# Fifty steps of a hand-written order put elsewhere, in a kernel that joins linear attention to a squared-ReLU layer

## The chip, the core and the metric

The kernel runs on one core of a Trainium2 chip. The core has five engines that work at the same time, each through its own queue in program order: TensorE (PE in the profile, its weight loads PEld), VectorE (DVE), ScalarE (ACT), GpSimd (POOL) and SyncE (SP), which here only issues DMAs. They wait for one another by semaphores. The metric is the time on the device in microseconds, lower is better.

## The reference

```python
# r, k, v: [4 batches, 8 heads, 768 steps, 48];  w, u: [8, 48]
for t in range(S):
    cur = einsum('bhd,bhe->bhde', u * k[t], v[t])
    y[t] = einsum('bhd,bhde->bhe', r[t], state + cur)
    state = w * state + einsum('bhd,bhe->bhde', k[t], v[t])
x = y.transpose(0, 2, 1, 3).reshape(3072, 384)
h = maximum(x @ w_in, 0)          # w_in  384 x 2048
out = (h * h) @ w_out             # w_out 2048 x 384
```

A recurrence over 768 steps gives 3072 rows of 384 numbers; each row then goes through two matrix products with a squared ReLU between them. Inputs and output are float32; the kernel multiplies in bf16.

## The kernel before

**Units and groups.** The recurrence is cut into 24 units, each 128 steps of one batch with all 8 heads (`UNITS` gives batch and chunk). Inside a unit it is done with matrix products, from unit to unit of a batch by a carried state. Units go in pairs through the dense layer: group g holds units 2g and 2g+1, except that units 22 and 23 are the groups 11 and 12 alone.

**Steps.** All work is a list of some 950 steps in one string, `ORDER`. A step is written `name.unit:engine/buffers`; `F1.8.2:P/1` is step F1 of group 8, slice 2, on TensorE into PSUM bank 1. The letters are P TensorE, D VectorE, A ScalarE, G GpSimd, S SyncE. A loop walks through the string and issues each step to its engine. So the string sets the order in each queue; between the queues only data, buffers and semaphores count. The steps that matter here, by unit i or group g:

- `ld.r`, `ld.k`, `ld.v` (L328): DMAs that bring 192 KB each. `rh`, `kh` (L347, L344): r and k times powers of w, in bf16. `XB` (L411): both transposed by a DMA.
- `P0`, `P1`, `du`, `dv` (L350, L354, L357, L362): the products r k, times u, summed over a head, times v: the term `cur`. `vb` (L259 or L257): v in bf16.
- `A` (L418): one product per head, eight matmuls of 48 rows, into two banks. `Bm` (L426): one of these banks times the mask, to SBUF.
- `Y` (L486 state part, L488 in-unit part): the output of the unit, in one bank. `xs` (L519): that plus dv, to bf16. `X` and `xTc` (L533, L257/L259), or the DMA `xX` (L540): xs transposed, x for the dense layer.
- `U`, `ts`, `S` (L508, L525, L528): the next state. `S` overwrites `S0W`, the state in bf16 of that batch, which `Y` of the same unit reads.
- `F1.g.s` (L549): six or twelve matmuls from x of the group into one bank. `re` (L571 on ScalarE, L573 on VectorE): ReLU of that bank into one of six `hr` buffers. `sq` (L578, L580): its square into one of 28 `hq` buffers.
- `F2.i.q` (L589): four matmuls from two squares of the group; four of them, q = 0 to 3, make the output of unit i in one bank. `os` copies it to SBUF, `out` writes it (L642). Unit 23 is done in two halves, `Fh`, `oh`, `outh` (L603, L257, L617).

**Buffers.** PSUM has 8 banks; a step that writes a bank waits until the step that reads what stood there is done. The same holds for `hr`, `hq`, `rk` and all the others; the number behind the slash says which buffer of its kind a step takes.

```python
    for step in ORDER.split():
        ...
        for h, j in zip(held, given):
            slot[h] = int(j)
        getattr(Do, name)(E[eng], *at)
```

Of the kernel before, what the change touches and what calls it, by code (L numbers as in the profile page):

```python
# [71 lines left out]
rh.17:G/1 F2.10.1:P/6 re.5.4:A/2 xs.12:D/2 xX.12:S/2 F2.11.0:P/2 os.9:D/1 sq.5.4:A/21 P0.16:G/0 XB.17:S/3 ts.13:D/1
Y.13:P/1 kh.16:D/5 F2.10.3:P/6 rh.16:G/5 F2.10.2:P/6 xs.13:D/3 out.5:S du.15:D/4 ld.k.18:S/4 F2.10.0:P/6 P1.16:G
ld.r.21:S/3 A.15:P/7/5 A.14:P/0/3 ld.r.19:S/2 Bm.15.0:D/5 dv.15:G F2.11.1:P/2 ld.r.18:S/5 Bm.15.1:D/7 S.13:G X.13:P/7
F2.11.3:P/2 xTc.13:A/2 Bm.14.0:D/4 Y.15:P/5 vb.14:G/7 du.14:D/0 F1.6.3:P/1 kh.19:G/0 xs.15:D/4 xX.15:S/0 ld.v.16:S/1
F1.6.2:P/7 re.6.3:A/0 Bm.14.1:D/6 F1.6.6:P/0 out.9:S out.6:S os.8:D/3 re.6.2:A/1 ld.r.20:S/4 sq.6.3:D/17 Y.14:P/5
re.6.6:A/3 P0.21:G/3 dv.14:D du.17:D/2 F1.6.1:P/1 XB.16:S/2 os.10:A/4 F1.6.4:P/4 S.12:G xs.14:D/0 F1.6.5:P/7
ld.k.20:S/5 rh.19:G/0 U.15:P/0 F1.6.7:P/6 re.6.5:A/4 ld.v.17:S/0 ts.15:D/1 X.14:P/3 S.15:G F1.6.0:P/5 re.6.7:A/5
xTc.14:D/0 P0.19:D/2 sq.6.2:A/20 sq.6.6:A/22 F1.7.7:P/7 XB.19:S/4 F1.7.6:P/0 re.6.4:D/2 sq.6.7:A/23 U.14:P/6 rh.21:G/3
out.8:A F1.7.5:P/3 re.7.6:D/0 kh.18:G/4 ld.r.23:S/6 vb.16:A/1 du.16:D/3 F1.7.0:P/4 sq.6.5:A/24 rh.20:G/6 re.6.0:D/1  # L80
F1.7.2:P/0 re.7.7:A/3 rh.18:D/4 ld.v.19:S/3 sq.6.4:A/25 F1.7.4:P/5 re.7.2:A/5 sq.7.2:A/5 F2.13.3:P/7 re.7.4:D/4
# [15 lines left out]
F1.9.2:P/7 re.9.2:A/2 du.22:D/2 F1.9.7:P/5 sq.9.6:A/12 du.21:D/1 F2.17.3:P/2 out.15:G out.12:G re.9.7:A/1 dv.21:G
F2.17.0:P/2 sq.9.3:A/15 vb.22:D/7 dv.23:G re.9.5:A/3 Y.20:P/7 Bm.21.0:D/2 F1.9.1:P/5 re.9.4:A/5 dv.22:D S.19:G
sq.9.5:A/8 F2.17.2:P/2 xs.20:D/0 sq.9.2:A/21 sq.9.4:D/17 Y.21:P/1 xX.20:S/0 sq.9.0:A/20 F2.17.1:P/2 xs.21:D/1
sq.9.7:A/7 F2.19.1:P/3 re.9.1:A/0 xX.21:S/0 F2.18.2:P/6 os.17:A/3 sq.9.1:A/9 A.23:P/0/7 A.22:P/1/5 os.16:A/0  # L100
Bm.23.0:D/4 F2.18.1:P/6 Bm.22.0:D/7 F2.18.3:P/6 Bm.22.1:D/5 F2.18.0:P/6 F2.19.0:P/3 Y.22:P/4 F1.10.2:P/2 re.10.2:D/3
# [5 lines left out]
sq.11.2:A/25 F1.10.7:P/6 re.10.6:A/3 F2.22.2:P/0 sq.10.6:A/4 re.10.7:D/2 re.12.0:A/5 F2.20.2:P/1 sq.11.1:D/5
sq.10.7:D/10 sq.12.0:A/14 F1.12.3:P/7 sq.12.1:D/18 F2.20.3:P/1 re.12.3:A/0 F2.20.0:P/1 Fh.23.2.0:P/4 os.20:A/5
# [585 lines left out]
```

## Time and profile before

| what | value |
| --- | --- |
| runs shown | 168.78, 169.06, 170.26 us, median 169.06 |
| the profiled execution | 168.3 us, of which span 166.5 us |
| busy, share of the span | PE 96%, DVE 79%, ACT 62%, POOL 60% |
| granted clock of TensorE | 1.0 throughout |
| instructions | 4501 |

The span runs from the first to the last recorded instruction. The views used: the page (busy shares, 40 slices, the chain that ended last), the timeline of one engine (start and length of each instruction or run of like ones, in brackets the idle time ahead of it and what ended it), and the table of stretches (columns: length, then busy time of PE, PEld, DVE, ACT, POOL with the number of instructions in brackets, then clock, DMA share, GB/s; of a single line it gives PE and PEld alone). An instruction belongs to a step by its place in its engine's order; `x12` in a row of L589 is three F2 steps.

### The profile page before, as it was taken

To read this page: it belongs to the slowest core of one execution; us is meant where nothing else is said; L and a number is where in the kernel's file an instruction comes from. 1 tells how busy PE (TensorE), PEld (TensorE's weight loads), DVE (VectorE), ACT (ScalarE), POOL (GpSimd) and SP (SyncE) were. 2 spreads that over 40 slices of the span, in tenths; PEclk is the share of its full clock that TensorE was granted. 3 is DMA by queue.
4 is the path that set the end of the run, shared out by engine and by line. 5 is a ranking of instruction groups with operands and counts; after the bars stand their busy time and mean duration, and the time that the engine had idled before them with its cause. 6 is when DMAs were issued, how large, how long until landed. Compare 5 with 4: busy or idle time off the path is not lost.

```text
span 166.5 us, 4501 instructions
## 1 busy us (share of the span) xinstructions
PE 160.1 (96%) x1772; PEld 120.4 (72%) x1772; DVE 132.3 (79%) x254; ACT 102.6 (62%) x193; POOL 100.3 (60%) x124
## 2 busy tenths in 40 slices
PE   4898999999999999999999999999999999999993
...
PEclk9999999999999999999999999999999999999999
...
GB/s 131 322 234 192 201 186 198 206 204 172 178 194 201 164 188 200 171 187 193 179 220 127 221 215 186 201 214 183 200 147 139 241 78 22 66 127 0 2 144 96
DMA packets 97713, 28.02 MB, mean 168 GB/s; under 512 B 92538, under 2 KB 97404, under 8 KB 97692
## 3 DMA queue, kind: packets, MB, share of 16 engines
...
q0 software_dynamic: 3072, 4.33, 13.2%
q10 hardware_dynamic: 892, 1.18, 3.1%
q8 instruction: 14, 0.23, 0.5%
q14 instruction: 7, 0.06, 0.1%
...
## 4 chain that ended last, share of the span: by engine, by line
PE 91%; DMA 4%; DVE 1%; ACT 1%; issue 1%; ACTq 0%; DVEq 0%
PE bank L549 37%; PE bank L589 35%; PE bank L418 3%; DMA xT<-xs 2%; PE bank L488 2%; DMA urow<-in_u_dram 2%; PE bank L486 2%; PE bank L371 2%; PE bank L533 2%; PE bank L603 2%; PE bank L508 1%; DVE Bm L399 1%; PE bank L278 1%; PE bank L561 1%; PE bank L391 1%; PE bank L405 1%
## 5 line engine op out<-in xcount | busy, mean ns | idle before, releaser
L589 PE MATMUL bank<-W,hq 128*128 128x384 bf16 x368 | 68.4, 326 | 0.0
L549 PE MATMUL bank<-xT,W 128*128 128x256 bf16 (+1 forms) x612 | 68.3, 264 | 0.1
L571 ACT ACTIVATE hr<-bank 128x512 bf16<-128x512 f32 x68 | 39.4, 594 | 35.1 <-PE bank L549 33.4
L549 PEld LDWEIGHTS <-W 128*128 128x128 bf16 x612 | 54.8, 98 | 8.4 <-issue 0.4
L589 PEld LDWEIGHTS <-hq 128*128 128x128 bf16 x368 | 33.7, 98 | 18.7
L578 ACT ACTIVATE hq<-hr 128x512 bf16<-128x512 bf16 x70 | 40.9, 626 | 5.6 <-DVE hr L573 4.7
L426 DVE TENSOR_TENSOR Bm<-bank,maskJT 128x512 bf16<-128x512 f32 x40 | 25.4, 679 | 2.8 <-PE bank L418 2.8
L573 DVE TENSOR_SCALAR hr<-bank 128x512 bf16<-128x512 f32 x28 | 18.7, 682 | 7.3 <-PE bank L549 4.8
L354 POOL TENSOR_TENSOR P<-P,ub 128x384 f32<-128x384 f32 x15 | 16.4, 1095 | 9.1 <-DVE P L350 8.7
L362 POOL TENSOR_TENSOR dv<-ldv,du 128x384 f32<-128x384 f32 (+1 forms) x18 | 15.7, 886 | 7.4 <-issue 3.8
L347 POOL TENSOR_TENSOR rk<-ldr,Wt 128x384 bf16<-128x384 f32 x15 | 15.6, 1043 | 2.2 <-DMA ldr<-in_r_dram 2.2
L580 DVE TENSOR_TENSOR hq<-hr 128x512 bf16<-128x512 bf16 x26 | 14.2, 560 | 2.3 <-ACT hr L571 2.1
L350 POOL TENSOR_TENSOR P<-ldr,ldk 128x384 f32<-128x384 f32 x13 | 13.3, 1023 | 2.6 <-DMA ldr<-in_r_dram 1.4
L344 POOL TENSOR_TENSOR rk<-ldk,Wk 128x384 bf16<-128x384 f32 x12 | 12.4, 1039 | 2.8 <-DMA ldk<-in_k_dram 2.3
L357 DVE TENSOR_REDUCE du<-P 128x8 f32<-128x384 f32 x24 | 12.8, 542 | 1.0 <-POOL P L354 0.9
L519 DVE TENSOR_TENSOR xs<-bank,dv 128x384 bf16<-128x384 f32 x20 | 10.9, 550 | 2.0 <-POOL dv L362 0.7
L259 POOL CAST vb<-ldv 128x384 bf16<-128x384 f32 x10 | 6.3, 626 | 10.3 <-DMA ldv<-in_v_dram 10.3
L528 POOL TENSOR_TENSOR S0W<-ts,WLm 128x384 bf16<-128x384 f32 x10 | 10.6, 1062 | 1.0 <-DVE ts L525 0.9
L259 DVE COPY os<-bank 128x384 f32<-128x384 f32 x11 | 6.0, 550 | 6.5 <-PE bank L589 6.3
L525 DVE TENSOR_TENSOR ts<-bank,S0W 128x384 f32<-128x384 f32 x16 | 8.8, 549 | 2.4 <-PE bank L508 1.1
L488 PE MATMUL bank<-vb,Bm 128*128 128x48 bf16 x160 | 9.5, 183 | 0.0
L488 PEld LDWEIGHTS <-Bm 128*128 128x128 bf16 x160 | 8.2, 96 | 1.3 <-DVE xs L519 0.4
(90 smaller groups left out, 166.5 us busy)
## 6 DMA issues: line engine op xcount, KB each, us to landing
...
```

The costliest lines, as they stand in the source:

```text
L347: e.tensor_mul(rk[slot[f"rk{i}"]][:, 0, :, 0:D], loaded("r", i), Do.factor("t", i % 2 if i < PAIRED else 2))
L350: e.tensor_mul(P0b[slot[f"P{i}"]], loaded("r", i), loaded("k", i))
L354: e.tensor_mul(t, t, bank("bu")[:, 0 : H * D].rearrange("p (h d) -> p h d", h=H) if i in EARLY_U else ub)
L362: e.tensor_mul(dv_of(i) if i < PAIRED else dvb[slot[f"dv{i}"]], loaded("v", i), t)
L426: e.tensor_mul(Bmb[slot[f"Bm{i}{h}"]], heads(bank(f"bA{i}{h}"), 128), mask_b)
L488: e.matmul(y[:, hc, D * h : D * (h + 1)], m[h][:, hc, :], vb[:, 2 * hc + h, :], start=(c == 0), stop=True, skip_group_check=True,)
L549: e.matmul(hp[:, fi, :], W1[f // 4][:, c, 256 * (f // 2 % 2) : 256 * (f // 2 % 2 + 1)].rearrange("p (m j) -> p j m", j=2)[:, f % 2, :], xt ...
L571: e.activation(hr, hp, AF.Relu)
L573: e.tensor_scalar_max(hr, hp, 0.0)
L578: e.activation(hq, hr, AF.Square)
L580: e.tensor_mul(hq, hr, hr)
L589: e.matmul(bank(f"bO{i}")[:, 0:d_model], hqb[slot[f"hq{g},{f // m}"]][:, at : at + L], W2[q][:, f % 4, :], start=(seen[i] == 1 and f % 4 = ...
```

## The change

Steps stand at other places in the string, three are on another engine, and some have other banks. No step is added or taken away, no function is changed. What each queue sees:

- **TensorE**: F2.3.2 ahead of Y.4; U.7 ahead of F2.5.1; F2.5.2 and F1.3.3 ahead of F1.3.1; A.10 from ahead of A.8 to behind X.9; F2.7.2 ahead of F2.7.0; Y.10 ahead of X.11; U.16 later, behind F1.7.1, and A.17 right after it, F2.12.1, F1.7.3 and F2.13.0 between it and A.16; F2.12.2 and F1.8.7 ahead of F1.8.2; F2.16.0 between A.20 and A.21; A.22 ahead of A.23; F1.10.2 ahead of F2.19.0, F1.10.5 earlier; F1.10.4, F1.10.6 and F2.20.1 ahead of F1.11.1, F1.11.2 earlier; Fh.23.3.0 ahead of Fh.23.1.1.
- **VectorE**: xs.4 ahead of du.5; S0.4 behind os.1; du.7 ahead of os.3; S.6 ahead of P0.10; xs.11 ahead of P1.13; du.13, S.8, xs.13, Bm.15.1, du.17, sq.6.0, P0.18, du.23 and xs.22 elsewhere by a step or a few; vb.17 ahead of sq.7.6 and ts.16.
- **ScalarE**: sq.0.1, re.4.3 and sq.4.1 come from VectorE; sq.3.7 from behind re.3.5 to behind sq.3.6.
- **GpSimd**: kh.13 from behind dv.9 (ahead of S.9) to behind P0.13; vb.12 ahead of S.10; S.11 behind dv.13; rh.17, rh.16; kh.18 ahead of S.15, P1.19 behind it; rh.20 and P1.18 behind P0.20; dv.18 ahead of vb.20, P1.20 behind it; P1.23 ahead of P1.22; dv.23 and out.15 ahead of vb.21.
- **SyncE**: the same order.

The core of the diff, places cut out:

```diff
-Y.4:P/0 P1.5:G du.5:D/0 F2.3.2:P/6 sq.1.2:A/15 ld.v.7:S/6 ld.k.9:S/0 xs.4:D/4 F2.0.0:P/4 vb.5:A/5 F2.3.0:P/6 Y.5:P/0
+F2.3.2:P/6 Y.4:P/0 P1.5:G sq.1.2:A/15 ld.v.7:S/6 ld.k.9:S/0 xs.4:D/4 du.5:D/0 F2.0.0:P/4 vb.5:A/5 F2.3.0:P/6 Y.5:P/0
...
-Bm.9.0:D/3 ld.v.12:S/4 dv.9:G sq.3.5:A/7 Bm.11.1:D/5 F1.3.6:P/0 Bm.11.0:D/7 sq.3.4:A/3 du.8:D/4 kh.13:G/4 A.10:P/5/7
-A.8:P/4/6 re.3.6:A/5 F2.7.0:P/2 Bm.8.0:D/0 sq.3.6:A/9 ld.k.12:S/5 ld.r.15:S/7 Y.9:P/1 vb.11:A/2 F2.7.2:P/2 Bm.8.1:D/1
-dv.8:D S.9:G vb.10:A/3 ld.k.14:S/7 F2.6.3:P/3 out.4:A P1.10:G Y.8:P/4 xs.9:D/3 F2.7.3:P/2 U.10:P/0 xs.8:D/4 P0.13:G/0
-X.9:P/6 Bm.10.1:D/4 X.8:P/1 F2.6.2:P/3 xTc.8:A/0 xTc.9:D/0 du.11:D/0 rh.12:G/0 Y.11:P/4 du.10:D/2 dv.10:G out.0:S
-F1.4.7:P/7 dv.11:G Bm.10.0:D/6 F1.4.6:P/6 ld.v.13:S/5 re.4.7:A/0 P1.13:D ld.r.14:S/6 F1.4.3:P/1 xs.11:D/0 re.4.6:A/1
-ld.v.15:S/6 du.13:D/1 F2.7.1:P/2 rh.15:G/6 ld.k.15:S/6 ts.10:D/1 F1.4.4:P/5 re.4.4:A/4 XB.13:S/5 kh.12:G/0 X.11:P/7
-Y.10:P/6 F1.4.1:P/4 S.10:G xs.10:D/1 sq.4.4:A/4 F1.4.5:P/5 re.4.3:D/3 ld.k.17:S/0 sq.4.6:D/2 X.10:P/0 F1.4.0:P/1
...
+ld.v.12:S/4 dv.9:G sq.3.5:A/7 Bm.11.1:D/5 F1.3.6:P/0 Bm.11.0:D/7 sq.3.4:A/3 du.8:D/4 A.8:P/4/6 re.3.6:A/5 F2.7.2:P/2
+F2.7.0:P/2 Bm.8.0:D/0 sq.3.6:A/9 sq.3.7:A/5 ld.k.12:S/5 ld.r.15:S/7 Y.9:P/1 vb.11:A/2 Bm.8.1:D/1 dv.8:D S.9:G
+vb.10:A/3 ld.k.14:S/7 F2.6.3:P/3 out.4:A P1.10:G Y.8:P/4 xs.9:D/3 F2.7.3:P/2 U.10:P/0 xs.8:D/4 P0.13:G/0 kh.13:G/4
+X.9:P/6 A.10:P/5/7 Bm.10.1:D/4 X.8:P/1 F2.6.2:P/3 xTc.8:A/0 xTc.9:D/0 du.11:D/0 rh.12:G/0 Y.11:P/4 du.10:D/2 dv.10:G
+out.0:S F1.4.7:P/7 dv.11:G Bm.10.0:D/6 F1.4.6:P/6 ld.v.13:S/5 re.4.7:A/0 xs.11:D/0 P1.13:D ld.r.14:S/6 F1.4.3:P/1
+re.4.6:A/1 ld.v.15:S/6 F2.7.1:P/2 rh.15:G/6 ld.k.15:S/6 ts.10:D/1 F1.4.4:P/5 re.4.4:A/4 XB.13:S/5 kh.12:G/0 Y.10:P/6
+X.11:P/7 F1.4.1:P/4 xs.10:D/1 sq.4.4:A/4 F1.4.5:P/5 re.4.3:A/3 ld.k.17:S/0 sq.4.6:D/2 X.10:P/0 F1.4.0:P/1 xTc.10:A/1
...
-XB.18:S/1 F2.11.2:P/2 ts.14:D/0 re.7.0:A/2 sq.6.0:D/9 U.16:P/0 F2.13.2:P/7 re.7.5:A/5 P1.21:D re.6.1:A/1 P0.18:D/4
-F1.7.1:P/5 sq.7.6:D/3 sq.6.1:A/7 ld.v.18:S/2 ld.v.20:S/5 P1.18:G F2.12.1:P/6 vb.17:D/0 sq.7.7:A/26 F1.7.3:P/4
-re.7.1:A/0 P1.19:G F2.13.0:P/7 ts.16:D/1 sq.7.0:A/27 sq.7.1:D/0 ld.v.21:S/4 re.7.3:A/1 A.17:P/3/1 dv.16:G A.16:P/5/0
...
+XB.18:S/1 F2.11.2:P/2 ts.14:D/0 re.7.0:A/2 F2.13.2:P/7 re.7.5:A/5 re.6.1:A/1 P0.18:D/4 F1.7.1:P/5 U.16:P/0 sq.6.1:A/7
+ld.v.18:S/2 ld.v.20:S/5 A.17:P/3/1 F2.12.1:P/6 P1.21:D vb.17:D/0 sq.7.6:D/3 sq.7.7:A/26 F1.7.3:P/4 re.7.1:A/0 P1.19:G
+rh.21:G/3 F2.13.0:P/7 ts.16:D/1 sq.7.0:A/27 sq.7.1:D/0 ld.v.21:S/4 re.7.3:A/1 dv.16:G A.16:P/5/0 Bm.17.1:D/2
...
-U.18:P/7 Y.18:P/0 S.17:D F1.8.2:P/1 du.18:D/4 F2.12.2:P/6 dv.18:G ts.19:D/0 F1.8.7:P/3 xs.19:D/3 xX.19:S/2 P0.23:G/0
+U.18:P/7 Y.18:P/0 S.17:D du.18:D/4 F2.12.2:P/6 dv.18:G vb.20:G/4 P1.20:G ts.19:D/0 F1.8.7:P/3 F1.8.2:P/1 xs.19:D/3
...
-A.20:P/1/5 S.18:G A.21:P/6/2 Bm.20.1:D/1 Bm.20.0:D/0 F2.16.0:P/4 vb.21:G/6 kh.22:D/5 Bm.21.1:D/3 F2.16.1:P/4 XB.22:S/2
+re.9.6:A/5 ts.18:D/1 A.20:P/1/5 S.18:G Bm.20.1:D/1 Bm.20.0:D/0 F2.16.0:P/4 A.21:P/6/2 kh.22:D/5 Bm.21.1:D/3 du.22:D/2
...
-re.10.5:D/5 Y.23:P/4 sq.10.5:D/22 F2.19.2:P/3 xs.23:D/3 re.10.3:A/4 sq.10.3:A/23 xX.23:S/1 sq.10.2:A/0 F1.11.1:P/7
-out.17:G F1.11.0:P/6 F1.10.4:P/0 out.16:G re.11.1:D/1 F2.21.1:P/5 re.11.0:A/0 F1.10.6:P/4 re.10.1:A/5 sq.11.0:D/27
-re.10.4:D/4 F1.11.3:P/2 sq.10.1:D/1 sq.10.4:A/6 F1.12.1:P/7 re.11.3:D/3 F1.11.2:P/6 sq.11.3:D/3 F2.20.1:P/1
...
+re.10.5:D/5 Y.23:P/4 sq.10.5:D/22 F2.19.2:P/3 xs.23:D/3 re.10.3:A/4 sq.10.3:A/23 xX.23:S/1 sq.10.2:A/0 F1.10.4:P/0
+F1.10.6:P/4 F2.20.1:P/7 F1.11.1:P/6 out.17:G F1.11.0:P/5 out.16:G re.11.1:D/1 F1.11.2:P/2 F2.21.1:P/6 re.11.0:A/0
+re.10.1:A/5 sq.11.0:D/27 re.10.4:D/4 F1.11.3:P/5 sq.10.1:D/1 sq.10.4:A/6 F1.12.1:P/1 re.11.3:D/3 sq.11.3:D/3
```

More of the change, by code (lines that the diff above doesn't have):

```diff
@@ L72 @@
[L72 to L81, printed above, removed]
@@ L97 @@
[L97 to L101, printed above, removed]
@@ L107 @@
[L107 to L110 removed]
+A.9:P/6/4 A.11:P/1/2 P0.11:D/2 P1.11:G sq.3.2:A/27 F2.6.0:P/3 ld.r.12:S/4 Bm.9.1:D/2 re.3.5:A/3 F2.6.1:P/3 Bm.9.0:D/3
```

76 lines of the change are left out of this document (46 added, 30 removed).

## The prediction

> **What bounds the kernel now.** I read the page first, then the table of stretches, then TensorE's timeline step by step.
>
> ```profile
> PE 160.1 (96%) x1772; PEld 120.4 (72%) x1772; DVE 132.3 (79%) x254; ACT 102.6 (62%) x193; POOL 100.3 (60%) x124
> PE   4898999999999999999999999999999999999993
> PEclk9999999999999999999999999999999999999999
> PE 91%; DMA 4%; DVE 1%; ACT 1%; issue 1%; ACTq 0%; DVEq 0%
> 64.00:72.00 8.00, 8.00 (x99) 6.40 (x97) 7.25 (x15) 3.30 (x7) 7.36 (x9) 1.00 0.79 169
> ```
>
> TensorE is busy 96% of the span at a full clock, its idle slices are the first few and the last one, and 91% of the chain is its own work. So the end moves by what happens to TensorE's queue: waits that close, waits that open, and work that becomes dearer. The other engines matter only where TensorE waits for them.
>
> The busy share hides short waits, since a matmul is drawn for some 0.2 us after it starts and covers the gap behind it. So I go by starts, from one step to the next.
>
> ```profile
> 44.77 1.46 PE L589 MATMUL bank<-W,hq 128*128 128x384 bf16 x8
> 46.07 1.63 PE L549 MATMUL bank<-xT,W 128*128 128x256 bf16 x12
> ```
>
> Two F2 steps of four matmuls take 46.07 - 44.77 = 1.30 us, 0.65 each. Against this price three places stand out after 25 us (before that only one square and one bank are changed).
>
> ```profile
> 33.75 2.11 PE L589 MATMUL bank<-W,hq 128*128 128x384 bf16 x12
> 35.88 0.37 PE L488 MATMUL bank<-vb,Bm 128*128 128x48 bf16 x8
> ...
> 34.80 0.55 DVE L357 TENSOR_REDUCE du<-P 128x8 f32<-128x384 f32 x1 [0.94 <-POOL P L354]
> 35.27 0.55 DVE L519 TENSOR_TENSOR xs<-bank,dv 128x384 bf16<-128x384 f32 x1
> ...
> 116.67 0.21 PE L486 MATMUL bank<-S0W,rkT 128*128 128x96 bf16 x1
> 117.29 0.55 PEld L549 LDWEIGHTS <-W 128*128 128x128 bf16 x6 [0.20 <-DMA xT<-xs]
> ...
> 144.27 0.81 PE L589 MATMUL bank<-W,hq 128*128 128x384 bf16 x4
> 145.08 2.15 PE L549 MATMUL bank<-xT,W 128*128 128x128 bf16 x30
> ```
>
> **The change: waits that close.** (1) F2.3.2, F2.0.0 and F2.3.0 should take 3 x 0.65 = 1.95 us, but Y.5 begins 35.88 - 33.75 = 2.13 after the first: it waited 0.18. It writes bank 0, which xs.4 has to read first, and xs.4 ends at 35.27 + 0.55 = 35.82 because it stands in VectorE's queue behind du.5, which sat 0.94 until GpSimd's P1.5. The change puts xs.4 ahead of du.5, and F2.3.2 ahead of Y.4. Y.4's results then come at about 34.6, xs.4 ends near 35.2, and Y.5 arrives at 35.70. **-0.18.** The next that is late is F1.2.5 behind os.2; it keeps its place and its wait.
>
> (2) Y.18 begins at 116.67; a Y step takes 0.37 (below, 71.17 to 71.54), so F1.8.2 should start at 117.04. It starts at 117.29, and the row names the transpose that brings x of 16/17. The change puts F2.12.2 (0.65) ahead of the first F1 of that group, more than the wait. **-0.25.**
>
> (3) F2.19.2 takes 145.08 - 144.27 = 0.81 instead of 0.65: F1.11.1 waits for x of 22. Now F1.10.4, F1.10.6 and F2.20.1 go first (two times 0.655, by the 12 matmuls from 71.54 to 72.85 below, and 0.65), and xs.22 goes ahead of re.10.2 on VectorE, so that its transpose is issued earlier too. F2.20.1's squares sq.10.2 and sq.10.3 are ready before it by the same order of queues. **-0.16.**
>
> **Work that becomes dearer.** A.10 leaves A.8, A.17 leaves A.16, and F2.16.0 goes between A.20 and A.21. In the trace every A stands beside another one.
>
> ```profile
> 81.20 1.46 PE L589 MATMUL bank<-W,hq 128*128 128x384 bf16 x8
> 82.59 0.62 PE L418 MATMUL bank<-rkT 48*128 48x128 bf16 x16
> 83.15 1.80 PE L589 MATMUL bank<-W,hq 128*128 128x384 bf16 x10
> ...
> 82.59:82.83 0.24, 0.23 (x9) 0.24 (x10) 1.00 0.93 160
> 82.83:83.15 0.32, 0.32 (x14) 0.21 (x8) 1.00 0.96 194
> ```
>
> The two F2 steps ahead of a pair take 82.59 - 81.20 = 1.39 instead of 1.30: a run-in of 0.09. Of the pair's 0.56 the first A takes 0.24 and the second 0.32 (the last two rows count L418 alone; weights are loaded in only 0.21 of the second stretch): a run-out of 0.08. The pair pays both once. Apart, each A pays them: 0.17 per pair split, three pairs, **+0.51.** No lone A of this form is in the trace, so the ends are 0 (a pair's cost stays a pair's) and 0.6.
>
> The Trainium skill's page "TensorEngine Tiling (Array Packing)", Key Properties, says that a change of the tiling mode, not of the tile alone, drains TensorE; an A has 48 rows where its neighbours have 128. By that rule every lone A drains twice and the sum is the +0.51; without it, it would be 0. The two gaps in the rows agree with it.
>
> **A wait that opens.** kh.13 goes from before S.9 to behind P0.13 in GpSimd's queue, and Y.10 goes ahead of X.11 on TensorE.
>
> ```profile
> 61.72 0.83 POOL L362 TENSOR_TENSOR dv<-ldv,du 128x384 f32<-128x384 f32 x1
> 63.05 1.00 POOL L344 TENSOR_TENSOR rk<-ldk,Wk 128x384 bf16<-128x384 f32 x1 [0.50 <-PE bank L418]
> 64.12 1.00 POOL L528 TENSOR_TENSOR S0W<-ts,WLm 128x384 bf16<-128x384 f32 x1
> 65.08 1.32 POOL L354 TENSOR_TENSOR P<-P,ub 128x384 f32<-128x384 f32 x1
> 68.33 1.93 POOL L362 TENSOR_TENSOR dv<-ldv,du 128x384 f32<-128x384 f32 x2
> ...
> 62.28 0.62 PE L418 MATMUL bank<-rkT 48*128 48x128 bf16 x16
> 63.49 0.21 PE L486 MATMUL bank<-S0W,rkT 128*128 128x96 bf16 x1
> 63.82 0.21 PE L488 MATMUL bank<-vb,Bm 128*128 128x48 bf16 x2
> 71.00 0.33 PE L533 MATMUL bank<-identity,xs 128*128 128x128 bf16 x3
> 71.17 0.21 PE L486 MATMUL bank<-S0W,rkT 128*128 128x96 bf16 x1
> 71.54 1.47 PE L549 MATMUL bank<-xT,W 128*128 128x256 bf16 x12
> 72.85 0.22 PE L533 MATMUL bank<-identity,xs 128*128 128x128 bf16 x1
> ...
> 68.77 0.80 DVE L354 TENSOR_TENSOR P<-P,ub 128x384 f32<-128x384 f32 x1
> 70.30 0.56 DVE L519 TENSOR_TENSOR xs<-bank,dv 128x384 bf16<-128x384 f32 x1 [0.72 <-POOL dv L362]
> 71.81 0.56 DVE L519 TENSOR_TENSOR xs<-bank,dv 128x384 bf16<-128x384 f32 x1
> ```
>
> Today kh.13 (63.05) fills the time in which S.9 could not run anyway: S.9 overwrites the state that Y.9 reads until 63.82 + 0.21 = 64.03, and starts at 64.12. From there GpSimd runs without a pause S.9, P1.10, P0.13, rh.12, dv.10, dv.11 to 68.33 + 1.93 = 70.26, and xs.11 starts 0.04 later, after 0.72 of waiting. In the new order GpSimd idles up to S.9, and kh.13's 0.96 (64.12 to 65.08, for S.9 of the same length) lies in the row that xs.11 waits for. A.8 starts at 62.28 - 0.18 = 62.10 and takes 0.32; F2.7.2 and F2.7.0 1.30; Y.9 starts at 63.72 and ends 0.54 later, as now, at 64.26. S.9 at 64.35, dv.11 out at 64.35 + 6.14 + 0.96 = 71.45. One thing is saved: P1.13 now ran beside dv.11, which took 1.93 - 0.83 = 1.10 for dv.10's 0.83; as P1.13 now stands behind xs.11, I take off 0.27: 71.18. xs.11 ends at 71.78, X.11 can start 0.06 later (35.82 to 35.88 above), at 71.84. TensorE is there at 71.00 - 0.18 + 0.17 + 0.37 for Y.10 = 71.36. **+0.48.** Ends: if P1.10 takes 1.00 instead of the 1.32 drawn, 0.32 goes and 0.16 is left; if the 0.27 isn't saved, 0.75.
>
> Behind xs.11 in VectorE's queue stand P1.13, ts.10 and xs.10, and X.10 waits for the last. With 0.80, 0.55 and 0.56, each overlapping the next by 0.08, xs.10 ends at 71.70 + 0.72 + 0.47 + 0.56 = 73.45 and X.10 can start at 73.51; TensorE gets there at 71.84 + 0.17 + 1.31 = 73.32. **+0.19.** Ends: 0, and 0.74 if P1.13 meets GpSimd as P1.12 did.
>
> ```profile
> 76.87 1.35 DVE L354 TENSOR_TENSOR P<-P,ub 128x384 f32<-128x384 f32 x1
> ```
>
> The Trainium skill's "SBUF — State Buffer", Who interferes with whom, says that a VectorE instruction with two SBUF inputs and a GpSimd one that reads SBUF hold a shared port exclusively, the later one waiting for the whole earlier. P1.13 would be issued into GpSimd's rh.15; by that rule it would lose what is left of rh.15, about 0.4 ahead of its own 0.55, 0.15 more than my 0.80, and the sum would be 0.15 higher. The rows of P1.13 and P1.12 agree in kind.
>
> **At nothing.** Bank numbers: each new bank was read out at least one step ahead. sq.0.1, re.4.3 and sq.4.1 go to ScalarE (3.30 of 8 us busy at 64 to 72), and VectorE gets time back. The moves of kh.18, P1.19, rh.20, P1.18, P1.20, dv.18 and dv.23 on GpSimd have readers well behind them in the order, and dv.18 comes earlier. SyncE's queue keeps its order, loads and transposes alike; the one DMA issue that moves is out.15 on GpSimd, ahead of vb.21, which Y.21 needs several steps later. If a cover were gone, TensorE would wait for the rest of one such operation, under 1 us. The end: oh.23.0 can start one short step earlier, but oh.23.1 still closes behind Fh.23.0.1; 0.
>
> **The sum**: -0.18 - 0.25 - 0.16 + 0.51 + 0.48 + 0.19 = **+0.59 us**. The profiled execution took 168.3 (span 166.5); it becomes 168.9 with a span of 167.1. That run is 0.76 below the median of the runs shown, so I add to the median: 169.06 + 0.59 = 169.65, given as 169.7.
>
> **The rivals.** (a) GpSimd recovers: without P1.10's stretch X.11 waits 0.16 and, with P1.13 as short, X.10 not at all: 169.65 - 0.32 - 0.19 = 169.1. For it: GpSimd's durations are the least steady. Against: seven steps in a row would have to run unhindered.
>
> (b) A lone A costs no more than half a pair: 169.65 - 0.51 = 169.1. For it: no row shows one. Against: the gaps on both sides of the pair.
>
> (c) The three waits don't close, the change not doing what its words say: 169.65 + 0.59 = 170.2. For it: what releases Y.5 and the two F1 steps is inferred. Against: each now has 0.4 us or more of other work ahead.
>
> (d) Slower: the landing of ld.v.17. vb.17 goes ahead of sq.7.6 in VectorE's queue.
>
> ```profile
> 105.43 0.41 DVE L580 TENSOR_TENSOR hq<-hr 128x512 bf16<-128x512 bf16 x1
> 106.55 0.37 DVE L259 CAST vb<-ldv 128x384 bf16<-128x384 f32 x1 [0.70 <-DMA ldv<-in_v_dram]
> 106.29 0.58 ACT L571 ACTIVATE hr<-bank 128x512 bf16<-128x512 f32 x1
> 107.33 0.62 PE L418 MATMUL bank<-rkT 48*128 48x128 bf16 x16
> ```
>
> It waits for that load until 106.55. Now sq.7.6 (0.41) follows it, re.7.1 (0.58) needs sq.7.6's buffer, and A.16 needs re.7.1's bank: 106.55 + 0.29 + 0.41 + 0.05 + 0.58 + 0.06 = 107.94. TensorE comes to A.16 at 107.33 + 0.24 + 0.17 + 0.66 (the sum up to there) = 108.40. So it decides from a landing 0.46 later than drawn; one 2 us later, my choice of a bad case, costs 1.54: 171.2. Against: nothing on that queue has moved.
>
> **How the numbers follow.** The forecast 0.55, (a) 0.15, (b) 0.1, (c) 0.08, (d) 0.08, unnamed 0.04. (a) and (b) together give 168.6; both upper ends of the new waits give 169.65 + 0.27 + 0.55 = 170.5; with (c) at 170.2 and the spread of single runs (168.78 to 170.26) I take **168.5 to 170.7**, which leaves out (d) and the unnamed. Over 1%, about what a measurement of this kernel can tell from no change, is 1.69 us. All the closed waits together are 0.59, so faster by that has only part of the unnamed, 0.03; slower has (d) and a share of the upper ends, 0.11; the same, 0.86.
>
> **What would show it.** Right: Y.5, F1.8.7 and F1.11.1 start without a gap; A.10, A.17 and A.20 alone take 0.32 with 0.09 ahead; GpSimd idles before S.9, dv.11 ends past 71 and X.11 starts about 0.5 after TensorE could. Wrong: a lone A without gaps, dv.11 out by 70.8, or TensorE waiting at A.16 or anywhere else for more than 0.3.

## The result, and the profile after

The changed order takes **170.7 us** (median of 12 runs, 169.8 to 172.72), the order of before on the same chip 169.2 (12 runs, 168.43 to 170.26). The ratio is 1.0096, 95% interval 1.0071 to 1.012: some 1.6 us slower, where the forecast was 0.6. Every ratio below is, like this one, against the order of before on the same chip, with its 95% interval in brackets. The ratios leave slow executions out, and the profiles of e2 (172.03 us) and e15 (172.84 us), which are of such executions, are not read. The profiled execution took 170.77 us with a span of 169.1. The page's busy line and the first line of its chain, of the changed kernel:

```profile
PE 162.6 (96%) x1772; PEld 121.6 (72%) x1772; DVE 134.2 (79%) x251; ACT 104.0 (61%) x196; POOL 100.8 (60%) x124
...
PE 66%; DVE 8%; DMA 8%; POOL 7%; ACT 4%; issue 2%; SPq 2%; ACTq 0%; POOLq 0%; DVEq 0%
```

TensorE is still busy 96% of the span, with 2.5 us more of "work": the drawn ends of matmuls cover part of the gaps. The chain tells it better. TensorE's share fell from 91% to 66%: it now runs through VectorE, GpSimd, a DMA and ScalarE, each of which TensorE waits for somewhere.

A span compares badly here. TensorE's timeline, first dense matmuls, of before, of before run again (e1, below), and of the changed kernel:

```profile
16.06 1.11 PE L561 MATMUL bank<-xT,W 128*128 128x128 bf16 x16
```
```profile
16.61 0.55 PE L561 MATMUL bank<-xT,W 128*128 128x128 bf16 x7
```
```profile
16.92 0.27 PE L561 MATMUL bank<-xT,W 128*128 128x128 bf16 x2
```

The same order starts its dense work 0.55 apart in two executions. A second profile of the changed order (e11) starts at 16.06 too, so the 0.9 between 16.06 and 16.92 belongs to neither order. From that first matmul to the last, the two profiles of before take 147.60 and 147.27 us, the two of the changed order 149.41 and 149.41. Gone through step by step as in the prediction (the time to the next step's start, less the step's price; for a split pair, what its two A's take apart less the 0.65 that the pair took), the difference lies here:

| TensorE's lost time, us | before | again (e1) | changed | again (e11) |
| --- | --- | --- | --- | --- |
| Y.5 | 0.18 | 0 | 0 | 0 |
| F1.8.2 | 0.25 | 0 | 0 | 0 |
| F1.11.1 | 0.17 | 0.17 | 0 | 0 |
| three split pairs | 0 | 0 | 0.62 | 0.62 |
| X.11 | 0 | 0 | 0.42 | 0.38 |
| X.10 | 0 | 0 | 0.22 | 0.23 |
| A.16 | 0 | 0 | 0.66 | 0.80 |
| T.5, X.5, F1.2.0 | 0.06 | 0.06 | 0.51 | 0 |
| F1.5.6 | 0 | 0 | 0 | 0.50 |

**X.11.** Timelines of the changed kernel: GpSimd, then VectorE, then TensorE (they answer to the prediction's rows from 63.05 on, 70.30 and 71.00).

```profile
65.68 1.38 POOL L528 TENSOR_TENSOR S0W<-ts,WLm 128x384 bf16<-128x384 f32 x1 [2.13 <-PE bank L488]
67.02 0.99 POOL L354 TENSOR_TENSOR P<-P,ub 128x384 f32<-128x384 f32 x1
67.98 0.99 POOL L350 TENSOR_TENSOR P<-ldr,ldk 128x384 f32<-128x384 f32 x1
68.93 1.00 POOL L344 TENSOR_TENSOR rk<-ldk,Wk 128x384 bf16<-128x384 f32 x1
69.89 1.00 POOL L347 TENSOR_TENSOR rk<-ldr,Wt 128x384 bf16<-128x384 f32 x1
70.85 1.61 POOL L362 TENSOR_TENSOR dv<-ldv,du 128x384 f32<-128x384 f32 x2
```
```profile
72.50 0.56 DVE L519 TENSOR_TENSOR xs<-bank,dv 128x384 bf16<-128x384 f32 x1 [2.00 <-POOL dv L362]
72.97 0.86 DVE L354 TENSOR_TENSOR P<-P,ub 128x384 f32<-128x384 f32 x1
```
```profile
73.12 0.34 PE L533 MATMUL bank<-identity,xs 128*128 128x128 bf16 x3 [0.26 <-DVE xs L519]
```

GpSimd idles 2.13 ahead of S.9, then kh.13 (68.93) stands in the row, dv.11 ends at 72.46, and xs.11 waits 2.00 for it, not 0.72 as before. X.11 starts 0.06 behind xs.11's end. Of the 0.42 TensorE really lost, the row shows 0.26 in brackets: the rest lies under the drawn end of Y.10.

**A.16.** VectorE, GpSimd, ScalarE and TensorE of the changed kernel:

```profile
108.37 0.36 DVE L259 CAST vb<-ldv 128x384 bf16<-128x384 f32 x1 [0.66 <-DMA ldv<-in_v_dram]
108.65 1.05 DVE L580 TENSOR_TENSOR hq<-hr 128x512 bf16<-128x512 bf16 x1
```
```profile
108.42 1.00 POOL L362 TENSOR_TENSOR dv<-ldv,du 128x384 f32<-128x384 f32 x1 [2.01 <-DMA ldv<-in_v_dram]
```
```profile
109.79 0.60 ACT L571 ACTIVATE hr<-bank 128x512 bf16<-128x512 f32 x1 [1.78 <-DVE hq L580]
```
```profile
107.39 0.40 PE L418 MATMUL bank<-rkT 48*128 48x128 bf16 x8
107.72 0.82 PE L589 MATMUL bank<-W,hq 128*128 128x384 bf16 x4
...
109.03 0.81 PE L589 MATMUL bank<-W,hq 128*128 128x384 bf16 x4
110.44 0.40 PE L418 MATMUL bank<-rkT 48*128 48x128 bf16 x8 [0.59 <-ACT hr L571]
110.77 1.47 PE L589 MATMUL bank<-W,hq 128*128 128x384 bf16 x8
```

One load, ld.v.17, releases vb.17 on VectorE and dv.17 on GpSimd together. Behind vb.17 sq.7.6 takes 1.05 instead of 0.41, re.7.1 follows, and A.16 starts at 110.44; TensorE could have started it at 109.03 + 0.65 + 0.10 = 109.78. The A rows and those behind them also show the lone A: 107.72 - 107.39 = 0.33 and 110.77 - 110.44 = 0.33 for eight matmuls, the 0.24 of a first A in a pair plus a run-out of 0.09.

### The profile page after: what moved, and what is told of

Its sections match the earlier page's. It is cut to its first block, busy times and chain, and to the rows that moved or that the text cites. A ratio compares the mean times of both kernels' runs of the same rounds, so it can differ in the third digit from the quotient of the medians.

```text
span 169.1 us, 4502 instructions
## 1 busy us (share of the span) xinstructions
PE 162.6 (96%) x1772; PEld 121.6 (72%) x1772; DVE 134.2 (79%) x251; ACT 104.0 (61%) x196; POOL 100.8 (60%) x124
## 3 DMA queue, kind: packets, MB, share of 16 engines
q10 hardware_dynamic: 892, 1.18, 3.0%
## 4 chain that ended last, share of the span: by engine, by line
PE 66%; DVE 8%; DMA 8%; POOL 7%; ACT 4%; issue 2%; SPq 2%; ACTq 0%; POOLq 0%; DVEq 0%
PE bank L589 25%; PE bank L549 24%; DMA ldr<-in_r_dram 4%; PE bank L371 2%; DMA ldv<-in_v_dram 2%; ACT hr L571 2%; DMA urow<-in_u_dram 2%; PE bank L418 2%; DVE P L354 2%; PE bank L603 2%; DVE Bm L426 1%; POOL dv L362 1%; PE bank L488 1%; PE bank L533 1%; SPq L328 1%
## 5 line engine op out<-in xcount | busy, mean ns | idle before, releaser
L571 ACT ACTIVATE hr<-bank 128x512 bf16<-128x512 f32 x69 | 40.1, 595 | 36.9 <-PE bank L549 32.2
L578 ACT ACTIVATE hq<-hr 128x512 bf16<-128x512 bf16 x72 | 41.9, 625 | 5.5 <-DVE hr L573 4.8
L573 DVE TENSOR_SCALAR hr<-bank 128x512 bf16<-128x512 f32 x27 | 17.9, 680 | 3.8 <-PE bank L549 3.8
L354 POOL TENSOR_TENSOR P<-P,ub 128x384 f32<-128x384 f32 x15 | 15.5, 1031 | 4.8 <-DVE P L350 4.2
L347 POOL TENSOR_TENSOR rk<-ldr,Wt 128x384 bf16<-128x384 f32 x15 | 16.3, 1089 | 0.1
L350 POOL TENSOR_TENSOR P<-ldr,ldk 128x384 f32<-128x384 f32 x13 | 14.1, 1084 | 3.7 <-DMA ldr<-in_r_dram 2.3
L580 DVE TENSOR_TENSOR hq<-hr 128x512 bf16<-128x512 bf16 x24 | 12.7, 545 | 1.4 <-ACT hr L571 1.3
L344 POOL TENSOR_TENSOR rk<-ldk,Wk 128x384 bf16<-128x384 f32 x12 | 13.1, 1099 | 1.2 <-DMA ldk<-in_k_dram 1.2
L257 ACT COPY xT<-bank 128x384 bf16<-128x384 bf16 x8 | 3.7, 480 | 8.6 <-PE bank L533 8.6
L259 POOL CAST vb<-ldv 128x384 bf16<-128x384 f32 x10 | 5.7, 568 | 5.6 <-DMA ldv<-in_v_dram 5.6
```

The lines of the kernel that those rows point to most:

```text
L344: e.tensor_mul(rk[slot[f"rk{i}"]][:, 1, :, 0:D], loaded("k", i), Do.factor("k", i % 2 if i < PAIRED else 2))
L347: e.tensor_mul(rk[slot[f"rk{i}"]][:, 0, :, 0:D], loaded("r", i), Do.factor("t", i % 2 if i < PAIRED else 2))
L350: e.tensor_mul(P0b[slot[f"P{i}"]], loaded("r", i), loaded("k", i))
L354: e.tensor_mul(t, t, bank("bu")[:, 0 : H * D].rearrange("p (h d) -> p h d", h=H) if i in EARLY_U else ub)
L571: e.activation(hr, hp, AF.Relu)
L573: e.tensor_scalar_max(hr, hp, 0.0)
```

## The experiments

**e1, before again, and three parts taken back alone.** e1 is the kernel before, without an edit.

> The kernel before, once more. The profiled span of the changed kernel was 169.1 us, 2.6 above before, though the medians differ by 1.5; its first dense step (L561) already began at 16.9 us where before had 16.1, ahead of every step that was moved. Theory: this 0.9 us is the start's own scatter (loads that land sooner or later), so this run starts L561 anywhere from 16.0 to 17.0, and from there to the last matmul it takes 147.6 us as in the first profile, within 0.2. Rival: the changed order delays the start by itself; then this run begins L561 at 16.1, within 0.1, and every kernel with the new order at 16.9.

It took 168.46 us. It began its dense work 0.55 later than before, as the theory allows, and took 147.27 from there, 0.33 less than before where the theory allowed 0.2: Y.5 and F1.8.2 started without a gap, F2.15.0 had a new one of 0.09, and F1.11.1 (0.17) and F1.2.5 (0.16) stood as before. Two of the three waits that the change was to close are not there in each execution.

```diff
e2, from changed:
-... sq.3.4:A/3 du.8:D/4 A.8:P/4/6 ...
+... sq.3.4:A/3 du.8:D/4 kh.13:G/4 A.8:P/4/6 ...
e3, from changed:
-... P1.21:D vb.17:D/0 sq.7.6:D/3 ...
+... P1.21:D sq.7.6:D/3 vb.17:D/0 ...
e4, from changed:
-F2.3.2:P/6 Y.4:P/0 P1.5:G sq.1.2:A/15 ... xs.4:D/4 du.5:D/0 F2.0.0:P/4
+Y.4:P/0 P1.5:G du.5:D/0 F2.3.2:P/6 sq.1.2:A/15 ... xs.4:D/4 F2.0.0:P/4
```

> The changed kernel with one step put back: kh.13 again ahead of S.9 in GpSimd's queue. Theory (GpSimd's queue reaches dv.11 too late): the gap of 0.42 us ahead of X.11 and that of 0.22 ahead of X.10 are gone (under 0.1 each), GpSimd idles under 0.8 us between dv.9 and S.9, and the time falls by 0.6 against the changed kernel, to 1.006 of before. The gap of 0.66 ahead of A.16 stays within 0.2, since the load that it hangs on moves along with TensorE. Rival 1: the gap comes from VectorE's order (xs.11 ahead of P1.13): it stays above 0.3 at X.11. Rival 2: the load lands when it lands; then what is won at X.11 is lost again at A.16, whose gap grows to 1.2, and the time stays at 1.0096.

> The changed kernel with vb.17 put back behind sq.7.6 in VectorE's queue (ahead of ts.16). Theory: sq.7.6 then runs before the load of v of 17 lands, in 0.4 us instead of 1.05, re.7.1 starts over 1 us earlier against TensorE, and the gap of 0.66 us ahead of A.16 falls under 0.15; time 0.6 less than the changed kernel, 1.006 of before. Rival 1: A.16 waits for ts.16 (bank 0) as much as for re.7.1, and ts.16 still stands behind vb.17: a gap of 0.3 or more stays. Rival 2: the load came late in that one profile only; the gap is gone, but the time is the changed kernel's, 1.0096.

> The changed kernel with the stretch from 33 to 40 us as before: Y.4 ahead of F2.3.2, du.5 ahead of xs.4. Theory (dv.5 took 1.30 instead of 0.64 us because it was issued just after GpSimd's P1.6 and xs.5 stood behind it): dv.5 takes under 0.8 again, the gaps of 0.19 ahead of X.5 and 0.16 ahead of F1.2.0 are gone, the gap of 0.18 ahead of Y.5 is back, in all 0.17 less than the changed kernel. Rival: the two gaps come from the later start of that execution, not from the order; they stay, Y.5's comes on top, and the time is 0.18 more than the changed kernel. In both cases the times alone may not tell, the steps' starts do.

e2: ratio 1.0032 (0.9996 to 1.0068), which takes in the theory's 1.006 and leaves out the second rival's 1.0096. In the five later kernels made from the change with kh.13 ahead of S.9 no profile has a gap at X.11 and one has a gap at X.10; of the six profiles with kh.13 behind P0.13, all have the one at X.10 and five the one at X.11. With the chain in the rows above, kh.13's place is the cause there; no profile that is read differs in it alone. e3: 1.0054 (1.0023 to 1.0085), the gap at A.16 gone, as its theory said; X.11 0.51 and X.10 0.22 are there, and new ones at F1.5.6 (0.51) and F1.7.4 (0.32). e4: 1.0076 (1.0043 to 1.0109); the gaps at X.5 and F1.2.0 are gone, as they are in e11 without any edit, and Y.5 had no gap with its old order either.

**The gap at F1.5.6** shows what kind of thing came new. VectorE and GpSimd of e11, the changed order's second profile:

```profile
75.89 1.35 DVE L528 TENSOR_TENSOR S0W<-ts,WLm 128x384 bf16<-128x384 f32 x1
77.17 1.35 DVE L350 TENSOR_TENSOR P<-ldr,ldk 128x384 f32<-128x384 f32 x1
78.44 1.35 DVE L347 TENSOR_TENSOR rk<-ldr,Wt 128x384 bf16<-128x384 f32 x1
79.71 1.35 DVE L354 TENSOR_TENSOR P<-P,ub 128x384 f32<-128x384 f32 x1
80.99 0.54 DVE L525 TENSOR_TENSOR ts<-bank,S0W 128x384 f32<-128x384 f32 x1
```
```profile
75.41 1.42 POOL L344 TENSOR_TENSOR rk<-ldk,Wk 128x384 bf16<-128x384 f32 x1 [0.57 <-DMA ldk<-in_k_dram]
76.79 1.31 POOL L350 TENSOR_TENSOR P<-ldr,ldk 128x384 f32<-128x384 f32 x1
78.18 1.19 POOL L354 TENSOR_TENSOR P<-P,ub 128x384 f32<-128x384 f32 x1
79.34 1.31 POOL L344 TENSOR_TENSOR rk<-ldk,Wk 128x384 bf16<-128x384 f32 x1
```

S.8, P0.14, rh.14 and P1.12 take 1.35 each, in step with a GpSimd instruction each; ts.11, a sum with one input in a PSUM bank, takes 0.54 and comes 0.5 too late for F1.5.6. In before (VectorE again), P0.14, rh.14 and S.8, then behind the other two, took 0.5 each:

```profile
75.00 1.01 DVE L350 TENSOR_TENSOR P<-ldr,ldk 128x384 f32<-128x384 f32 x2
75.94 0.55 DVE L347 TENSOR_TENSOR rk<-ldr,Wt 128x384 bf16<-128x384 f32 x1
76.41 0.55 DVE L528 TENSOR_TENSOR S0W<-ts,WLm 128x384 bf16<-128x384 f32 x1
```

This gap stood in 3 of the 11 profiles with S.8 and S.10 as changed, and in none of the 5 with them as before: too few to say that the new order brings it.

**Parts of the change put into before, parts taken out of it.**

```diff
e5, from before:
-A.10:P/5/7 A.8:P/4/6 ... X.9:P/6 Bm.10.1:D/4
+A.8:P/4/6 ... X.9:P/6 A.10:P/5/7 Bm.10.1:D/4
-F2.13.0:P/7 ... A.17:P/3/1 dv.16:G A.16:P/5/0
+A.17:P/3/1 F2.13.0:P/7 ... dv.16:G A.16:P/5/0
-A.20:P/1/5 S.18:G A.21:P/6/2 ... F2.16.0:P/4
+A.20:P/1/5 S.18:G ... F2.16.0:P/4 A.21:P/6/2
e6, from before; from A.20 on all as changed, but A.20 and A.21 together:
-Y.4:P/0 P1.5:G du.5:D/0 F2.3.2:P/6 ... xs.4:D/4 F2.0.0:P/4
+F2.3.2:P/6 Y.4:P/0 P1.5:G ... xs.4:D/4 du.5:D/0 F2.0.0:P/4
-F1.8.2:P/1 du.18:D/4 F2.12.2:P/6 ... F1.8.7:P/3
+du.18:D/4 F2.12.2:P/6 ... F1.8.7:P/3 F1.8.2:P/1
e7, from changed; GpSimd's queue there is S.15 rh.21 kh.18 rh.20 P1.18 P1.19 dv.16 again:
-... du.8:D/4 A.8:P/4/6 ...
+... du.8:D/4 kh.13:G/4 A.8:P/4/6 ...
-F2.12.1:P/6 P1.21:D vb.17:D/0 sq.7.6:D/3
+sq.7.6:D/3 ... F2.12.1:P/6 vb.17:D/0 P1.21:D
e8, from changed: A.10 back ahead of A.8, A.17 ahead of A.16, A.21 behind A.20
```

> The order of before, with only the three pairs of A taken apart (A.10 behind X.9, A.17 ahead of F2.13.0, A.21 behind F2.16.0). Theory: each lone A pays a run-in of 0.096 and a run-out of 0.095 that the pair paid once, so 0.19 a split and 0.56 to 0.57 in all, ratio about 1.0033, and no other gap is new: GpSimd's and VectorE's queues are those of before. Rival 1: the gaps around a lone A are there but swallow other small waits, so that the time does not move (ratio within 0.001 of 1). Rival 2: most of the 1.6 us that the change lost comes from the splits, since Bm.10, Bm.17 and Bm.21 come later or earlier and hold up others (ratio above 1.006).

> The order of before with only the edits that were to close waits: F2.3.2 ahead of Y.4 and xs.4 ahead of du.5; F1.8.2 behind F2.12.2 and F1.8.7; and the whole end from A.20 on as in the change (F1.10.4, F1.10.6, F2.20.1 ahead of F1.11.1), with A.21 beside A.20. Theory: the wait at F1.11.1 stood in both profiles of before (0.166, 0.168) and closes, the waits at Y.5 and F1.8.2 stood in one of the two only, so -0.17 for sure and -0.38 if they are there half the time: ratio 0.9978 to 0.999. Rival 1, the prediction's working: -0.59, ratio 0.9965. Rival 2: the end's edits open as much as they close (ratio 1.000 or more).

> The order of the change with kh.13 back ahead of S.9, vb.17 back behind sq.7.6, and GpSimd's S.15, rh.21, kh.18, rh.20, P1.18, P1.19 in the order of before; the three pairs of A stay apart. Theory: what the change lost beyond the splits are waits that TensorE has for a VectorE or GpSimd instruction which now stands later or runs into the other engine's; with the queues back these go and +0.56 - 0.17 = +0.39 is left, ratio about 1.0023, and no gap over 0.3 at X.11, X.10, A.16, F1.7.0, F1.7.4. Rival: the losses move on to other places of the order, as they did at F1.5.6 and F1.7.4 when one edit alone was taken back, and the ratio stays above 1.006.

> The order of the change with A.10 back beside A.8, A.17 beside A.16, A.21 beside A.20; all else as changed. Theory: 0.56 less than the change, so about 170.1 where the change has 170.7, ratio about 1.006. Rival 1: A.10 and A.8 together set kh.13 and S.9 no earlier, but TensorE, which now waits at X.11 anyway for xs.11, only waits longer, and only two of the splits come back: 0.38 less, ratio 1.0073. Rival 2: nothing comes back, ratio 1.0096.

e5: 1.0027 (0.9997 to 1.0056), so 0.46 where 0.56 was expected. By steps the three splits cost 0.62 in its profile: a lone A takes 0.10 ahead and 0.33, the pair took 0.65 with its run-in. So the theory holds by steps; the interval of the times just takes in 1. But "no other gap is new" was wrong. X.11 waited 0.24 here, with kh.13 where before has it. VectorE and GpSimd of e5:

```profile
66.71 0.69 DVE L426 TENSOR_TENSOR Bm<-bank,maskJT 128x512 bf16<-128x512 f32 x1 [0.50 <-PE bank L418]
...
68.67 1.93 POOL L362 TENSOR_TENSOR dv<-ldv,du 128x384 f32<-128x384 f32 x2 [0.61 <-DVE du L357]
```

Bm.10.1 waits for the A.10 that now comes later, and du.10 stands behind it. On GpSimd dv.10 waits for du.10, dv.11 stands behind dv.10, and xs.11 needs dv.11. So splitting this pair can have a price on VectorE too, which neither the prediction nor this expectation counted.

e6: 0.9977 (0.9948 to 1.0007), at the end of what was expected; the interval takes in the rival's 0.9965 as well as 1. It opened a wait, as VectorE's timeline of e6 shows:

```profile
35.14 0.54 DVE L357 TENSOR_REDUCE du<-P 128x8 f32<-128x384 f32 x1
35.72 0.63 DVE L362 TENSOR_TENSOR dv<-ldv,du 128x384 f32<-128x384 f32 x1
36.46 0.56 DVE L519 TENSOR_TENSOR xs<-bank,dv 128x384 bf16<-128x384 f32 x1
...
38.13 0.35 DVE L259 COPY xT<-bank 128x384 bf16<-128x384 bf16 x1
```

du.5 now stands behind xs.4, which waits for Y.4; dv.5, xs.5 and xTc.5 (38.13) come later, and F1.2.0 waits 0.17 for the last. In e5, with du.5 ahead, xs.5 starts at 36.10. Of the seven profiles with the edit four have this wait (0.17 to 0.56 with X.5's); of the nine without it, two have the one at Y.5 that it closes.

e7: 1.0081 (1.0046 to 1.0116): the theory's 1.0023 is out, and the number is the rival's. X.11 and X.10 were free, but 0.76 stood at A.16 and 0.56 at X.5 and F1.2.0. VectorE and TensorE of e7:

```profile
106.24 1.21 DVE L259 CAST vb<-ldv 128x384 bf16<-128x384 f32 x1 [0.82 <-DMA ldv<-in_v_dram]
107.37 1.18 DVE L354 TENSOR_TENSOR P<-P,ub 128x384 f32<-128x384 f32 x1
108.47 0.55 DVE L525 TENSOR_TENSOR ts<-bank,S0W 128x384 f32<-128x384 f32 x1
```
```profile
108.30 0.23 PE L418 MATMUL bank<-rkT 48*128 48x128 bf16 x1
109.07 0.38 PE L418 MATMUL bank<-rkT 48*128 48x128 bf16 x7 [0.55 <-DVE ts L525]
```

A.16 starts and stops after one matmul: its second bank, U.16's, is emptied by ts.16, which stands behind vb.17 (1.21 instead of 0.36) and P1.21 (1.18 instead of 0.55), both beside GpSimd. Two roads lead from that load to A.16, one for each bank; e7 closed one. e8: 1.0071 (1.0042 to 1.0099), 0.4 less than the change; the theory and both rivals lie inside the interval. A.16 waited 1.43 in its profile, behind the load again.

**Does it add up?**

```diff
e9, from e7, and Y.4, F2.3.2, du.5, xs.4 as in e4:
-P0.18:D/4 ... vb.17:D/0 P1.21:D
+P1.21:D P0.18:D/4 ... vb.17:D/0
e10, from e6, and Y.4, F2.3.2, du.5, xs.4 as in before:
-F1.2.5:P/4
+F1.2.5:P/7
e11, the changed order again: no edit
e12, from e9, and the A pairs joined as in e8
```

> As the run before with the queues taken back (kh.13, vb.17, GpSimd's S.15, rh.21, kh.18, rh.20, P1.18, P1.19 in the order of before), and now P1.21 back ahead of P0.18, and du.5 and F2.3.2 back ahead of xs.4 and behind Y.4; the three pairs of A stay apart. Theory: the 0.76 at A.16 that was left there came from ts.16, which empties A.16's second bank and stood behind P1.21 in VectorE's queue, and the 0.39 and 0.16 at X.5 and F1.2.0 from du.5 standing behind xs.4. Without them the splits are left, less the wait at F1.11.1 and half of that at F1.8.2: +0.56 - 0.17 - 0.12 = +0.27, ratio about 1.0016, and no gap over 0.3 at A.16 and X.5. Rival: the losses move on again to other places, ratio 1.006 or more.

> The order of before with three things: F1.8.2 behind F2.12.2 and F1.8.7; the end from A.20 on as in the change with A.21 beside A.20; and F1.2.5 into bank 7 instead of 4, so that it need not wait for os.2 (0.157 in every profile so far). VectorE's and GpSimd's queues up to A.20 are those of before. Theory: -0.17 at F1.11.1 and -0.16 at F1.2.5 for sure, -0.12 for F1.8.2 on the mean: -0.33 to -0.45, ratio 0.9973 to 0.998. Rival: closing F1.2.5's wait only moves it to the next step that needs os.2 or its square later, ratio 0.999 or more.

> The changed order again, for a second profile of it. Theory: the gaps that come from the order stand again, X.11 0.4 to 0.6, X.10 about 0.2, A.16 0.4 or more, F1.2.5 0.16, and the first dense step starts anywhere in 16.0 to 17.0; what comes from chance meetings of VectorE and GpSimd or of a load (T.5, X.5, F1.5.6, F1.7.4) may be there or not. Rival: A.16's wait was such a chance too and is under 0.1.

> As the first kernel of this set, and the three pairs of A joined again. What is left of the change: bank numbers, three steps on ScalarE, F1.8.2 and the end, and the smaller moves. Theory: these cost nothing, so -0.17 - 0.12 = -0.29, ratio about 0.998, and 0.56 less than the first kernel of the set. Rival: the rest costs by itself, ratio 1.002 or more.

e9: 1.0014 (0.9986 to 1.0043), 0.24 us where 0.27 was expected, and the rival's 1.006 is out. But the sum behind it is not shown: its profile still had 0.59 at A.16, where no gap over 0.3 was expected. e10's had 0.52 there; both are behind vb.17, in e10 with VectorE's queue of before. e10: 0.9983 (0.9952 to 1.0014); F1.2.5's wait is gone, no gain over before is shown, and the theory and its rival aren't told apart. e11 (170.0 us) has the waits of the order again, A.16 with them. e12 was expected at 0.998 and gave 1.0034 (0.9999 to 1.007), though its profile is free of all these gaps but F1.2.5's. That profile is of an execution of 168.59 us, 1.0 under the kernel's median, so it doesn't show what the others lost.

**The load.** A third set takes vb.17 out from ahead of all that A.16 needs.

```diff
e13, from e12; e15, from e10; e16, from changed (e14 is e12 again):
-vb.17:D/0 ... ts.16:D/1 ... sq.7.1:D/0 ... Bm.17.1:D/2
+ts.16:D/1 ... sq.7.1:D/0 ... Bm.17.1:D/2 vb.17:D/0
```

> The change with its waits taken back and its pairs joined (the last kernel of the set before), and vb.17 moved in VectorE's queue from ahead of ts.16 to behind Bm.17.1, so that nothing A.16 needs stands behind the load ld.v.17. Theory: the landing of that load scatters from under 106.4 to 108.4, and in about half of the executions ts.16 behind vb.17 holds A.16 for 0.5 or more; without that the ratio is about 0.998. Rival: the 1.0034 of the kernel without this edit has another cause, and the ratio stays at 1.002 or more.

> The same kernel as e12 once more (the change with its waits taken back and its pairs joined). Theory of the scatter: between 0.998 and 1.003, with executions at both ends. Rival, what is left of the change costs by itself: 1.003 or more again, with an interval above 1.

> As e10 (the order of before, with F1.8.2 behind F1.8.7, the end of the change, F1.2.5 in bank 7), and vb.17 moved behind Bm.17.1 in VectorE's queue. Theory: the 0.52 at A.16 in the profile of e10 goes where the load lands late; on the mean another 0.2, ratio about 0.997. Rival: late landings are rare in this order, and the ratio is that of e10, 0.998.

> The changed order with one edit: vb.17 from ahead of sq.7.6 and ts.16 to behind Bm.17.1 in VectorE's queue. Theory: the wait at A.16 (0.66 and 0.80 in two profiles) falls below 0.2, what is left being ts.16 behind P1.21; the time falls by about 0.6, ratio 1.0055 to 1.0065. Rival: the wait at A.16 comes from GpSimd's dv.17 stretching VectorE's steps, not from their standing behind the load, and half of it or more stays: ratio 1.008 or more.

e16: 1.0043 (1.002 to 1.0066), 0.9 less than the change and more than the 0.6 that was expected, which the interval takes in; the rival is out. VectorE of e16:

```profile
106.57 0.41 DVE L580 TENSOR_TENSOR hq<-hr 128x512 bf16<-128x512 bf16 x1
106.91 0.55 DVE L525 TENSOR_TENSOR ts<-bank,S0W 128x384 f32<-128x384 f32 x1
...
108.71 0.55 DVE L259 CAST vb<-ldv 128x384 bf16<-128x384 f32 x1
```

sq.7.6 takes 0.41 again, and A.16 starts at 108.85 without a wait. By the ratios one moved instruction gives back more than half of the loss. (X.11 did not wait in that profile, but X.9 ahead of it waited 0.36 instead.) e13: 0.9992 (0.9964 to 1.002); e14: 1.0012 (0.9982 to 1.0043) for e12's order, and the two intervals overlap widely, so its 1.0034 needs no cause of its own; whether the small rest of the change costs anything stays open. e15: 0.9993 (0.9963 to 1.0023), where 0.997 was expected: no better than e10. A likely reason, seen in e13's profile only: Bm.16.0 and Bm.16.1 then stand behind the load, Y.16 waits for them, and 0.29 is lost ahead of F2.15.0. No version is shown to beat before.

All profiles read, by where vb.17 stands: ahead of sq.7.6, A.16 waited in 4 of 4 (0.13, 0.66, 0.80, 1.43); behind sq.7.6 but ahead of ts.16, as in before, in 3 of 10 (0.52 to 0.76); behind both, in none of 2.

## Why the prediction was wrong

**The step that failed** is the wait at A.16, which the sum puts at nothing: GpSimd's moved steps under "At nothing", vb.17 ahead of sq.7.6 in rival (d) alone, at a chance of 0.08 and with a slack of 0.46 that wasn't there. The runs showed 0.66 and 0.80 us lost at A.16, and the prediction's own sign of being wrong, TensorE waiting there for more than 0.3.

**Right: the splits.** 0.51 forecast, 0.62 by steps, 0.46 by time, where the interval is wide.

**Right: X.11 and X.10.** 0.48 and 0.19 forecast, 0.38 to 0.42 and 0.22 to 0.23 measured. The chain was as written; S.9 took 1.38 and P1.10 0.99 where 1.00 and 1.32 were assumed; that the two errors nearly cancel (2.37 for 2.32) was luck. P1.13 took 0.86, not 0.80.

**Half right: the closed waits, (1) to (3).** All three are closed. But (1) and (2) were priced from the only execution shown, and Y.5's wait is there in 2 of 9 profiles, F1.8.2's in 1 of 3. (3) was there in 3 of 3. So -0.59 was, on the mean, about -0.17 - 0.08 - 0.04 = -0.29. And "the next that is late is F1.2.5" missed the next link of (1): du.5, put behind a step that waits for Y.4, delays dv.5, xs.5 and F1.2.0.

**Wrong: "At nothing".** The paragraph asked of GpSimd's moved steps only who reads their results and when. It did not ask which VectorE instruction they would run beside. With rh.20 and P1.18 put behind P0.20, GpSimd's queue is empty when ld.v.17 lands (idle 2.01 above) and dv.17 starts at that moment; before, P1.18, P1.19 and dv.16 stood ahead of dv.17. So it was in all four profiles with both edits: sq.7.6 took 1.05 each time. The Trainium skill's "SBUF — State Buffer", Who interferes with whom, says that the engine that issues first keeps the shared port for its whole instruction and the other is blocked. The rows agree: sq.7.6 0.41 alone, 1.05 beside dv.17. The page says that casts can take that port too, when their operands meet its conditions; vb.17 at 0.36 and at 1.21 agrees. I had used that rule for one moved step, P1.13, and for none of the others. What GpSimd's moved steps cost by themselves is not shown: no run has vb.17 ahead of sq.7.6 with GpSimd's queue of before, and with that queue vb.17 itself took up to 1.21 (e7, e10).

**Wrong: rival (d), by its slack.** Its mechanism, its place and its queue were right, at a chance of 0.08. It decided "from a landing 0.46 later than drawn", with two terms fixed that were not. Between the landing and A.16 were to lie 1.39; it was 110.44 - 108.37 = 2.07, of which 0.64 is sq.7.6's stretch. And the landing did not stay while TensorE came later: it came later too. SyncE's queue of before, then of the changed kernel:

```profile
99.03 3.37 SPq L411 DMA_TRANSPOSE rkT<-rk  x1
...
103.07 0.58 SPq L328 DMA_DIRECT2D ldv<-in_v_dram  x1
```
```profile
100.91 3.33 SPq L411 DMA_TRANSPOSE rkT<-rk  x1
104.28 0.58 SPq L328 DMA_DIRECT2D ldk<-in_k_dram  x1
104.90 0.58 SPq L328 DMA_DIRECT2D ldv<-in_v_dram  x1
```

ld.v.17 stands in order behind XB.16. The queue reached XB.16 1.88 later than in before (0.86 of it is the later first dense matmul), so the load was issued 1.83 later, and vb.17 started 3.5 after the issue in both. TensorE could have started A.16 2.21 later than in before (109.78 for 107.33 + 0.24 = 107.57), and the load landed 1.82 later (108.37 for 106.55). So the slack grew by 0.4, not by the 0.83 of the forecast. XB.16's issue itself took 2.17 (e6) to 3.69 (e9) from one profile to another. "Nothing on that queue has moved" was true of the order and false of the time. Without the stretch A.16 would have come 0.64 earlier and waited 0.02. That is worked out from rows, for the stretch was not varied alone; that the steps' standing behind the load is needed for the wait, e16 shows.

What was missed, on the mean of the two changed profiles: A.16 0.73, F1.5.6 or X.5 and its neighbours 0.45, and 0.20 because two of the waits to be closed stood in only one of the two profiles of before: 1.38. These profiles lie 1.97 us above the two of before, 1.38 more than the forecast's 0.59; the medians of the runs, with other chances in each, differ by 1.5, 0.9 more than forecast. Only A.16's part is tied to an edit by a run (e16, and e3); the 0.45 came and went with the order unchanged.
